# A convolution feeding two feed-forward layers: due dates of five convolutions put two slots earlier, their first step one slot earlier

## Chip, cores and metric

The kernel runs on one core of one Trainium2 chip. The metric is device time in microseconds (us), the median of several executions. One further execution was profiled, and all rows below come from it.

## What is computed

The reference, cut to the arithmetic (the input is 2 x 4096 tokens of 192 channels; all is in float32):

```python
# attn: causal depthwise convolution, 7 taps, softmax-normalised weights, 8 heads
out = np.einsum('hk,bskhg->bshg', w, x_unf)          # x_unf: 7 shifted copies of x
# layer 1, x (8192,192), w_in (192,2048), w_out (2048,192)
h = x @ w_in;  g = h * np.clip(h + 3.0, 0.0, 6.0) / 6.0;  y = g @ w_out
# layer 2, other weights
h = y @ w_in;  g = np.where(h > 0, h, np.exp(np.minimum(h, 0.0)) - 1.0);  out = g @ w_out
```

## The kernel before

**Tiling.** The 8192 tokens are cut into 16 blocks of 512 (256 of each batch entry). The 2048 inner columns of a layer are cut into 16 chunks of 128. One layer, one block and one chunk make a *slot*, `(l, b, f)`, and the list `slots` is the order of the program: first layer-1 blocks 0 and 1 interleaved (slots 0 to 31), then layer-1 blocks 2 to 5 (slots 32 to 95, 16 each), then layer-2 block 0 (96 to 111), layer-1 block 6 (112 to 127), and from there a layer-2 and a layer-1 block in turn, ending with layer-2 blocks alone. `at` gives the number of a slot. BOTH is 32, the first slot of block 2.

**A slot.** TensorE (PE) makes `h` from the block's operands (`mm1`, L452) and four slots later adds this slot's share to the outputs `p` (`mm2`, L492). Between them ScalarE (ACT) makes `u` from `h`, VectorE (DVE) makes the gate `g` from `u` and `h`, ACT rounds `g` to `gh`, and DVE makes the rest `gl = g - gh`. Products are split into high and low parts, so a slot has ten matmuls. From slot 36 on each matmul is done as two halves of 64 rows: the stream of lower halves runs eight matmuls ahead of that of upper halves, and the two alternate in one PE queue. `h` has three PSUM buffers, so `mm1` of slot s needs that `g` of slot s-3 is done.

**The operands.** `mm1` of a layer-1 block reads the tiles opA, opB, opC and opD. `conv(b)` makes them: two DVE transposes of the block's tokens (`squares`: xT from x_sq and xr_sq), twelve multiply-adds on DVE (`acc`, six of 512 and six of 256 columns; ACT starts each sum), then copies on ACT and subtractions on DVE: opA on ACT, opB on DVE, first halves of opC and opD on ACT, their other halves on DVE, then one more ACT copy each. `mm1` reads opA, opB, opA, opC, opD in this order, and an upper or a lower half may leave out one of the last two. The loads of a block's tokens are a job of their own (`feed`), in SyncE's (SP's) queue.

**The order of the work.** Instructions of each engine stand in the order in which the program issues them (up to slot 36 a scheduler may still exchange them; from there the order is as written). Convolutions and the decoding of weights are *jobs*. After the gate of every slot s, `run_jobs(s)` issues steps of those jobs that are wanted. A job has a first slot `a`, a due slot `e` and a number of steps n. It is finished outright once `s >= e - 2` (`e - 1` where e is not over 32); before that its steps are spread evenly, `done * (e - a) < n * (s - a + 1)`. In the slots before 36, instead, steps are issued where a budget of DVE and ACT work allows. For layer-1 block b, `conv(b)` has n = 22 steps, `a = t` and `e`, as set in these lines:

```python
    for b in range(2, NBLK):
        e = at[0, b, 0]
        if b <= RA:
            t = at[0, b - 1, 1]
        else:
            t = at[1, b - RA - 1, NF - 3]
            e = at[1, b - RA, NF - 3]
        job(feed(b), 1, t - 8, t - 7)
        job(whole(squares(b), conv(b)), 2 + CONV, t, e)
```

RA is 6. While layer-1 blocks 2 to 6 are computed, the weights of layer 2 are decoded too, which is more DVE and ACT work in the same slots.

Of the kernel before, what the change touches and what calls it, by code (L numbers as in the profile page):

```python
# [56 lines left out]
def conv_moe_moe2(ctx: ExitStack, tc: tile.TileContext, x, weight, w_in1, w_out1, w_in2, w_out2, out):  # L57
# [211 lines left out]
    def squares(b):  # L269
        for part, t in enumerate(x_sb.pop(b)):  # L270
            vec.transpose(out=halves(b, part), in_=t)
            yield
# [48 lines left out]
    def conv(b):  # L321
        opnd[0, b] = ring()
        yield from alternate(conv_main(b, taps_tensor if b < TENSOR_TAPS else taps_vector), conv_r(b))
# [12 lines left out]
    def feed(b):  # L336
        load_squares(b)
        yield
# [166 lines left out]
    at = {sl: i for i, sl in enumerate(slots)}  # L505
# [11 lines left out]
    def job(gen, n, a, e):  # L517

        jobs.append([e if callable(e) else lambda: e, a, gen, n, 0])
# [29 lines left out]
    def whole(*gens):  # L549
        for g in gens:  # L550
            yield from g
# [105 lines left out]
    job(weights, 0, 0, pace)  # L657
    job(conv(1), CONV, 0, at[0, 1, 0])
    for b in range(2, NBLK):
        e = at[0, b, 0]  # L660
        if b <= RA:
            t = at[0, b - 1, 1]
        else:
            t = at[1, b - RA - 1, NF - 3]
            e = at[1, b - RA, NF - 3]
        job(feed(b), 1, t - 8, t - 7)
        job(whole(squares(b), conv(b)), 2 + CONV, t, e)
    for b in range(NBLK):
        e = at[1, b, 0]
# [100 lines left out]
```

## Time and profile before

| what | us |
|---|---|
| median of three executions | 1200.68 (1200.63 to 1919.79) |
| the profiled execution | 1200.85 |
| its span, first to last instruction | 1199.1 |
| PE busy | 1173.4 (98%) |
| DVE busy | 943.7 (79%) |
| ACT busy | 931.4 (78%) |
| mean granted PE clock | 0.992 of full |

The span is what the rows count in; 1.75 us of the profiled execution lie around it. Busy time of PE is the time in which at least one matmul was shown; it says nothing of how many ran in it. A number in square brackets behind an instruction is the idle time of its engine just before it, and what ended it.

### The profile page before, as it was taken

What the parts mean: (1) busy time and instruction counts of PE and PEld (TensorE: products, weight loads), DVE (VectorE), ACT (ScalarE), POOL (GpSimd) and SP (SyncE); (2) the same over time, 40 slices, a digit from 0 to 9 for tenths busy, and PEclk for the clock granted to TensorE, in tenths of its full rate; (3) what the DMA queues carried; (4) which work ended last, traced back from release to release, by engine and by line L of the source; (5) the groups of instructions that cost most, each with busy time, mean ns of one, the idle gap of its engine ahead of it and who ended that gap; (6) DMA issues with size and microseconds to landing.
All of it is one profiled execution on the core that took longest, in us unless ns stands there. A gap on an engine that the chain in (4) does not pass through costs nothing.

```text
span 1199.1 us, 25137 instructions
## 1 busy us (share of the span) xinstructions
PE 1173.4 (98%) x9496; PEld 975.2 (81%) x9496; DVE 943.7 (79%) x1607; ACT 931.4 (78%) x1683; POOL 44.1 (4%) x490
## 2 busy tenths in 40 slices
PE   8999999999999999999999999999999999999997
PEld 6787677787898879878898778988889888987776
DVE  8999897897877778787787878778787766677774
ACT  6877676779687786968778697887969678888885
POOL 0000000000000000000000000000000000000000
PEclk9999998999999999999999999999999999999999
DMA  6331111100101001010000101001000000000001
GB/s 166 98 97 31 40 32 41 28 1 1 28 1 19 11 1 28 1 28 1 13 16 1 27 2 28 2 7 22 2 15 2 14 1 2 15 15 15 15 11 18
DMA packets 108091, 26.81 MB, mean 22 GB/s; under 512 B 99648, under 2 KB 106816, under 8 KB 107968
## 3 DMA queue, kind: packets, MB, share of 16 engines
q1 hardware_dynamic: 106320, 24.99, 9.9%
q8 instruction: 74, 1.21, 0.4%
q14 instruction: 49, 0.40, 0.1%
q10 hardware_dynamic: 1648, 0.20, 0.1%
HBM read 18.87 MB, written 6.29 MB: 21 GB/s over the span
## 4 chain that ended last, share of the span: by engine, by line
PE 86%; DVE 7%; ACT 5%; issue 1%; DMA 0%; SPq 0%; ACTq 0%; DVEq 0%
PE p L492 44%; PE h L452 41%; ACT u L51 2%; DVE g L51 2%; DVE acc L51 2%; DVE gl L51 2%; ACT gh L51 1%; ACT y L51 1%; PE psc L291 1%; DVE s L51 0%; ACT opC L51 0%; ACT s L51 0%; DMA x_sb<-in_x_dram 0%; DVE cw L51 0%; ACT opD L51 0%
## 5 line engine op out<-in xcount | busy, mean ns | idle before, releaser
L492 PE MATMUL p<-gh,wo 64*128 64x512 f32 (+1 forms) x2976 | 656.5, 394 | 0.2 <-ACT gh L51 0.2
L492 PE MATMUL p<-gl,wo 64*128 64x512 f32 (+1 forms) x1984 | 535.0, 394 | 0.0
L51 DVE SCALAR_TENSOR_TENSOR g<-u,h 128x512 f32<-128x512 f32 x512 | 350.8, 685 | 224.1 <-ACT u L51 220.4
L492 PEld LDWEIGHTS p<-gh,wo 64*128 64x128 f32 (+1 forms) x2976 | 463.1, 186 | 57.7 <-ACT gh L51 0.7
L492 PEld LDWEIGHTS p<-gl,wo 64*128 64x128 f32 (+1 forms) x1984 | 361.8, 186 | 37.9 <-DVE gl L51 0.3
L51 DVE TENSOR_TENSOR gl<-g,gh 128x512 fp32r<-128x512 f32 x512 | 350.5, 685 | 0.4 <-ACT gh L51 0.2
L51 ACT CAST gh<-g 128x512 fp32r<-128x512 f32 x512 | 311.8, 609 | 21.6 <-DVE g L51 21.3
L51 ACT ACTIVATE u<-h,three 128x512 f32<-128x512 f32 x256 | 176.2, 688 | 118.2 <-PE h L452 116.1
L452 PE MATMUL h<-opA,wi1h 64*128 64x512 f32 x512 | 199.7, 395 | 0.3
L452 PE MATMUL h<-opA,wi1l 64*128 64x512 f32 x512 | 199.2, 394 | 0.0
L452 PE MATMUL h<-opB,wi1h 64*128 64x512 f32 x512 | 198.1, 392 | 0.0
L452 PE MATMUL h<-opA,wi0h 64*128 64x512 f32 (+1 forms) x476 | 189.0, 401 | 3.1 <-ACT opA L51 1.7
L51 ACT ACTIVATE u<-h 128x512 f32<-128x512 f32 x256 | 152.6, 596 | 50.6 <-PE h L452 48.3
L452 PE MATMUL h<-opA,wi0l 64*128 64x512 f32 (+1 forms) x476 | 188.3, 399 | 0.0
L452 PE MATMUL h<-opB,wi0h 64*128 64x512 f32 (+1 forms) x476 | 187.0, 396 | 1.3 <-DVE opB L51 1.1
L51 ACT ACTIVATE u<-u 128x512 f32<-128x512 f32 x256 | 161.9, 632 | 8.1
L452 PE MATMUL h<-opC,wi0r 64*128 64x512 f32 (+1 forms) x366 | 144.9, 398 | 7.5 <-ACT opC L51 7.5
L452 PE MATMUL h<-opD,wi1r 64*128 64x512 f32 x384 | 149.3, 392 | 0.0
L452 PE MATMUL h<-opC,wi1r 64*128 64x512 f32 x384 | 149.3, 392 | 0.0
L452 PE MATMUL h<-opD,wi0r 64*128 64x512 f32 (+1 forms) x366 | 144.2, 396 | 0.0
L51 DVE SCALAR_TENSOR_TENSOR acc<-xT,taps,acc 128x256 f32<-128x256 f32 (+1 forms) x180 | 106.7, 602 | 0.6 <-ACT acc L51 0.5
L452 PEld LDWEIGHTS h<-opA,wi0h 64*128 64x128 f32 (+1 forms) x476 | 88.5, 186 | 21.3 <-DVE g L51 7.8
(83 smaller groups left out, 1255.0 us busy)
## 6 DMA issues: line engine op xcount, KB each, us to landing
raw<-in_moe_w_out_dram SPq DMA_DIRECT2D x16, 384.0 KB, 3.1
out_dram<-z SPq DMA_DIRECT2D x186, 32.0 KB, 1.6
raw<-in_moe_w_in_dram SPq DMA_DIRECT2D x7, 512.0 KB, 3.6
x_sq<-in_x_dram SPq DMA_DIRECT2D x112, 32.0 KB, 2.2
raw<-in_moe_w_in_dram SPq DMA_DIRECT2D x8, 256.0 KB, 4.1
xr_sq<-in_x_dram SPq DMA_DIRECT2D x56, 32.0 KB, 2.0
x_sb<-in_x_dram SPq DMA_DIRECT2D x4, 128.0 KB, 2.9
raw<-in_moe_w_in_dram SPq DMA_DIRECT2D x4, 128.0 KB, 4.1
```

The costliest lines, as they stand in the source:

```text
L51: return fn(*args, **kw)
L291: nc.tensor.matmul(ps[:, n * HB:(n + 1) * HB], diag[k], q[:, n, k:k + HB], start=k == 0, stop=k == K - 1)
L452: mm = nc.tensor.matmul(h, k, m[half], start=low and i == 0, stop=high and i == len(todo) - 1)
L492: nc.tensor.matmul(p, k, m[half], start=first and not end and k is not w0l, stop=last and end == 1)
```

## The change

The due slot of a convolution is two less, and for blocks 2 to 6 the first slot is one less. For blocks 7 to 15 `e` is set again in the `else` branch, so nothing changes there.

```diff
     for b in range(2, NBLK):
-        e = at[0, b, 0]
+        e = at[0, b, 0] - 2
         if b <= RA:
-            t = at[0, b - 1, 1]
+            t = at[0, b - 1, 0]
         else:
             t = at[1, b - RA - 1, NF - 3]
             e = at[1, b - RA, NF - 3]
```

What this moves, at three places. Numbers behind names are those of tiles; the same tile can have another number in the two kernels.

DVE at the first slots of block 2, in the kernel before: the last two of the twelve multiply-adds (acc0, acc1), the last steps of the operands, and the next gates. g_1063 is the gate of slot 31 and stands ten multiply-adds above; g_1123 is that of slot 32.

```order
L51 SCALAR_TENSOR_TENSOR acc0_1081<-xT0_1071,taps_96,acc0_1081 128x512
L51 SCALAR_TENSOR_TENSOR acc1_1083<-xT1_1074,taps_96,acc1_1083 128x256
L51 SCALAR_TENSOR_TENSOR cw_1029<-xw_1027,cw_1029 128x512
L51 TENSOR_TENSOR opB_1078<-acc0_1081,opA_1077 128x512
L51 TENSOR_TENSOR opC_1079<-acc1_1083,opD_1080 64x256
L51 TENSOR_TENSOR opD_1080<-acc1_1083,opC_1079 64x256
L51 TENSOR_TENSOR gl_1129<-g_1063,gh_1127 128x512
L51 SCALAR_TENSOR_TENSOR xw_1027<-xw_1027,cw_1029 128x512
L51 TENSOR_SCALAR cw_1156<-raw_957 128x384
L51 TENSOR_TENSOR yr_1158<-s1_1115,yr_1158 128x512
L51 SCALAR_TENSOR_TENSOR g_1123<-u_1124,h_1117 128x512
```

The same place in the changed kernel. Here g_1078 is the gate of slot 30, g_1097 that of slot 31 and g_1123 that of slot 32; eleven multiply-adds stand between the gate of slot 29 and g_1078.

```order
L51 SCALAR_TENSOR_TENSOR acc0_1041<-xT0_1031,taps_96,acc0_1041 128x512
L51 SCALAR_TENSOR_TENSOR acc1_1043<-xT1_1034,taps_96,acc1_1043 128x256
L51 SCALAR_TENSOR_TENSOR g_1078<-u_1079,h_1072 128x512
L51 TENSOR_TENSOR opB_1038<-acc0_1041,opA_1037 128x512
L51 TENSOR_TENSOR opC_1039<-acc1_1043,opD_1040 64x256
L51 TENSOR_TENSOR opD_1040<-acc1_1043,opC_1039 64x256
L51 TENSOR_TENSOR gl_1084<-g_1014,gh_1082 128x512
L51 TENSOR_TENSOR gl_1103<-g_1078,gh_1101 128x512
L51 SCALAR_TENSOR_TENSOR g_1097<-u_1098,h_1091 128x512
L51 TENSOR_TENSOR wi1r_90<-xw_959,wi1r_90 64x4x128
L51 SCALAR_TENSOR_TENSOR cw_1029<-xw_1027,cw_1029 128x512
L51 SCALAR_TENSOR_TENSOR g_1123<-u_1124,h_1117 128x512
```

The convolution moved ahead of the gates of slots 30 and 31, and some decoding (xw_1027, cw_1156) and the sum yr moved behind the gate of slot 32.

DVE ahead of block 3, whose first slot is 48. In the kernel before, g_1597 is the gate of slot 46 and g_1631 that of slot 47.

```order
L51 TENSOR_SCALAR cw_1572<-raw_1152 128x512
L51 TENSOR_TENSOR opB_1254<-acc0_1257,opA_1253 128x512
L51 SCALAR_TENSOR_TENSOR g_1597<-u_1598,h_1551 128x512
L51 TENSOR_TENSOR gl_1603<-g_1559,gh_1601 128x512
L51 TENSOR_TENSOR opC_1255<-acc1_1259,opD_1256 64x256
L51 TENSOR_TENSOR opD_1256<-acc1_1259,opC_1255 64x256
L51 SCALAR_TENSOR_TENSOR g_1631<-u_1632,h_1591 128x512
```

In the changed kernel g_1530 is the gate of slot 44 and g_1566 that of slot 45.

```order
L51 TENSOR_TENSOR opB_1254<-acc0_1257,opA_1253 128x512
L51 SCALAR_TENSOR_TENSOR g_1530<-u_1531,h_1492 128x512
L51 TENSOR_TENSOR gl_1536<-g_1500,gh_1534 128x512
L51 TENSOR_TENSOR opC_1255<-acc1_1259,opD_1256 64x256
L51 TENSOR_TENSOR opD_1256<-acc1_1259,opC_1255 64x256
L51 SCALAR_TENSOR_TENSOR g_1566<-u_1567,h_1524 128x512
L51 TENSOR_TENSOR gl_1572<-g_1530,gh_1570 128x512
L51 TENSOR_SCALAR cw_1579<-raw_1152 128x512
```

The last operand steps moved up past two gates. Ahead of blocks 4 and 5 they move in the same way.

PE at block 2, in the kernel before; p0_517 and p1_518 are outputs of block 1, gh_1046, gh_1067 and gh_1127 belong to slots 29, 30 and 31, and h_1117 is slot 32.

```order
L492 MATMUL p1_518<-gh_1046,wo0_91 128x512
L492 MATMUL p0_517<-gl_1048,wo0_91 128x512
L492 MATMUL p1_518<-gl_1048,wo0_91 128x512
L492 MATMUL p0_517<-gh_1067,wo0_91 128x512 x2
L492 MATMUL p1_518<-gh_1067,wo0_91 128x512
L492 MATMUL p0_517<-gl_1069,wo0_91 128x512
L492 MATMUL p1_518<-gl_1069,wo0_91 128x512
L492 MATMUL p0_517<-gh_1127,wo0_91 128x512 x2
L492 MATMUL p1_518<-gh_1127,wo0_91 128x512
L452 MATMUL h_1117<-opA_1077,wi0h_85 128x512
```

In the changed kernel gh_1082 and gl_1084 belong to slot 29, gh_1101 to slot 30; h_1117 and h_1137 are slots 32 and 33.

```order
L492 MATMUL p1_518<-gh_1082,wo0_91 128x512
L452 MATMUL h_1117<-opA_1037,wi0h_85 128x512
L452 MATMUL h_1137<-opA_1037,wi0h_85 128x512
L452 MATMUL h_1117<-opB_1038,wi0h_85 128x512
L452 MATMUL h_1117<-opA_1037,wi0l_86 128x512
L452 MATMUL h_1137<-opB_1038,wi0h_85 128x512
L452 MATMUL h_1137<-opA_1037,wi0l_86 128x512
L492 MATMUL p0_517<-gl_1084,wo0_91 128x512
```

The first matmuls of block 2 moved ahead of twelve matmuls on slots 29 to 31.

## Rows read from the trace of the kernel before

**Rows 1.** The page's first part: busy us, share of span, instructions.

```profile
PE 1173.4 (98%) x9496; PEld 975.2 (81%) x9496; DVE 943.7 (79%) x1607; ACT 931.4 (78%) x1683; POOL 44.1 (4%) x490
```

**Rows 2.** Stretches between gates: column names, then start:end, length, busy time and instructions.

```profile
core 0: us, PE busy (x) PEld busy (x) DVE busy (x) ACT busy (x) POOL busy (x), PEclk, DMA share, GB/s
94.12:105.06 10.94, 9.19 (x33) 6.73 (x32) 10.10 (x19) 6.46 (x13) 0.00 (x0) 0.85 0.00 1
105.06:144.27 39.21, 35.61 (x265) 27.94 (x265) 33.00 (x60) 27.56 (x52) 1.24 (x14) 0.95 0.26 55
144.27:186.05 41.78, 38.88 (x304) 30.59 (x302) 36.40 (x65) 29.23 (x55) 1.33 (x15) 0.93 0.12 34
186.05:226.05 40.00, 37.45 (x312) 28.84 (x310) 35.34 (x66) 27.79 (x52) 1.51 (x17) 0.99 0.19 40
...
94.12:262.09 167.97, 157.18 (x1212) 123.21 (x1212) 148.14 (x269) 118.37 (x220) 5.48 (x62) 0.96 0.14 31
...
262.09:1152.54 890.45, 889.83 (x7603) 749.53 (x7602) 682.17 (x1112) 712.95 (x1279) 35.25 (x400) 1.00 0.07 11
```

**Rows 3.** All waits of PE after 262.09: us in total, times, longest.

```profile
PE h L452 <- ACT opC L51: 0.4, 1, 0.4
PE p L492 <- ACT gh L51: 0.2, 1, 0.2
```

**Rows 4.** Timeline at block 2: start, length, instruction, idle time before it.

```profile
94.73 5.38 DVE L51 SCALAR_TENSOR_TENSOR acc<-xT,taps,acc 128x512 f32<-128x512 f32 x10
...
95.47 0.86 PE L492 MATMUL p<-gh,wo 128*128 128x512 f32 x3
...
99.74 0.62 ACT L51 CAST opA<-acc 128x512 fp32r<-128x512 f32 x1 [2.60 <-DVE acc L51]
...
100.41 0.96 PE L452 MATMUL h<-opA,wi0h 128*128 128x512 f32 x3 [1.75 <-ACT opA L51]
```

**Rows 5.** Timeline ahead of block 3, DVE and then PE.

```profile
134.03 0.69 DVE L51 SCALAR_TENSOR_TENSOR g<-u,h 128x512 f32<-128x512 f32 x1 [0.40 <-ACT u L51]
...
135.58 0.69 DVE L51 TENSOR_TENSOR opB<-acc,opA 128x512 fp32r<-128x512 f32 x1
137.08 0.69 DVE L51 SCALAR_TENSOR_TENSOR g<-u,h 128x512 f32<-128x512 f32 x1 [0.82 <-ACT u L51]
...
138.28 0.41 DVE L51 TENSOR_TENSOR opC<-acc,opD 64x256 fp32r<-64x256 f32 x1
...
136.32 0.50 PE L452 MATMUL h<-opB,wi0h 64*128 64x512 f32 x1 [0.37 <-DVE opB L51]
...
139.64 0.79 PE L452 MATMUL h<-opC,wi0r 64*128 64x512 f32 x1 [2.59 <-ACT opC L51]
```

**Rows 6.** Timeline ahead of blocks 4 and 5: one gate, then PE.

```profile
176.19 0.69 DVE L51 SCALAR_TENSOR_TENSOR g<-u,h 128x512 f32<-128x512 f32 x1
...
178.60 0.49 PE L452 MATMUL h<-opB,wi0h 64*128 64x512 f32 x1 [0.77 <-DVE opB L51]
...
181.01 0.79 PE L452 MATMUL h<-opC,wi0r 64*128 64x512 f32 x1 [1.68 <-ACT opC L51]
...
222.86 0.49 PE L452 MATMUL h<-opC,wi0r 64*128 64x512 f32 x1 [2.15 <-ACT opC L51]
```

**Rows 7.** Stretches of 10 us, columns as in Rows 2.

```profile
120.00:130.00 10.00, 10.00 (x86) 8.03 (x88) 10.00 (x20) 6.38 (x11) 0.35 (x4) 1.00 0.15 39
130.00:140.00 10.00, 7.03 (x56) 4.92 (x54) 7.90 (x15) 7.91 (x16) 0.26 (x3) 0.97 0.27 61
140.00:150.00 10.00, 10.00 (x76) 7.95 (x76) 7.12 (x14) 5.38 (x12) 0.35 (x4) 0.86 0.13 20
...
180.00:190.00 10.00, 8.98 (x54) 7.12 (x56) 4.01 (x9) 5.44 (x12) 0.27 (x3) 0.66 0.32 69
```

**Rows 8.** Loads of block 4's tokens in SP's queue, and their first reader.

```profile
105.08 2.08 SPq L266 DMA_DIRECT2D x_sq<-in_x_dram  x4
...
148.41 0.70 DVE L51 STREAM_TRANSPOSE xT<-x_sq 128x512 f32<-128x512 f32 x1
```

## Prediction

> **What bounds the kernel now.** I read the busy shares first. PE is busy for 1173.4 of 1199.1 us [rows 1], so at first sight there is little to win. The second view is the length of each block, taken from the first gate of one block to the first gate of the next. From 262.09 to 1152.54 there are 25 blocks in 890.45 us, 35.62 us each, and PE is idle for 0.62 us in all of them [rows 2]. That is a full PE: one block cannot be shorter without fewer matmuls. The list of PE's waits after 262.09 holds two, of 0.4 and 0.2 us [rows 3]. So anything to be won lies before 262.09, where layer-1 blocks 2 to 5 run one behind the other. There block 2 takes 39.21 us, block 3 41.78 and block 4 40.00 [rows 2], which is 3.59, 6.16 and 4.38 us more than 35.62. One more stretch stands out: from the gate of slot 31 to that of slot 32, the first of block 2, 10.94 us pass, where a slot costs about 35.62/16 = 2.2.
>
> The third view is the timeline at the start of each block. PE waits there for the operands that the convolution makes. At block 2 it idles 1.75 us for opA; ACT could not make opA before, since ten multiply-adds had held DVE for 5.38 us [rows 4]. At block 3 it idles 0.37 us for opB and 2.59 for opC [rows 5], at block 4 0.77 and 1.68, at block 5 2.15 [rows 6]. In each case the last operand step stands in DVE's queue behind a gate which itself waited for the next `u`: opC of block 3 runs at 138.28, behind the gate at 137.08 [rows 5]. The operands are late because of their place in the queue, not for want of their inputs.
>
> The fourth view is the clock. In 130 to 140 the granted clock is 0.97, in 140 to 150 0.86, in 180 to 190 0.66 [rows 7]: after the idle time at blocks 3 and 4 PE runs at 1.2 GHz for a while instead of 2.4. The loss is one minus the clock, times the length: (0.03 + 0.14) x 10 = 1.7 us at block 3 and 0.34 x 10 = 3.4 us at block 4.
>
> **What the change does, and its price.** Despite its wording it acts on five convolutions of blocks 2 to 6; for the others `e` is set again. No instruction is added or taken away. The operand steps of blocks 3, 4 and 5 go up by two gates, and the transposes and multiply-adds of each convolution close up by one to two slots. Two slots are 2 x 2.2 = 4.4 us, more than any of the waits. At block 3 the step that now runs at 138.28 would stand just ahead of the gate that ran at 134.03 [rows 5]; PE asked for opC about 139.64 - 2.59 = 137.05. I therefore take these operand waits as gone.
>
> What is late next is the gate. DVE works through its queue in order, so opB, opC and opD, 0.69 + 0.41 and about 0.4 more, or 1.5 us in all, now stand ahead of a gate two slots earlier. Behind that gate waits PE, because `h` has three buffers. Below, the price is nothing if DVE was idle ahead of these gates, and it was, for 0.40 and 0.82 us at 134.03 and 137.08 [rows 5]. Above, it is the whole 1.5 us, since ahead of block 4 the gate at 176.19 follows without any idle time [rows 6]. Also `u` of that slot now stands behind the last ACT copies of opC and opD, which wait for DVE. I take 1.5 - 0.4 = 1.1 us for each block, the bound less the smaller idle time.
>
> Block by block, with 35.62 us of matmuls as the floor:
> - Gate 31 to gate 32 (10.94 us): in the new order eleven multiply-adds, 11 x 0.538 = 5.9 us by the 5.38 for ten, stand between the gates of slots 29 and 30 and begin about two slots sooner. By the old times they begin at about 90.2 and end at 96.1; opA takes 0.62, so PE has it at 96.7 instead of 100.36. PE now reaches block 2 after the high-part matmuls of slot 29, at about 95.47 + 0.7 = 96.2, and waits 0.5 us instead of 1.75. The gate of slot 32 follows after about 5 to 6 us of queue (two gates, three operand steps, two `gl`, decoding), at 102.0 instead of 105.06. This is 3.1 us sooner; but xw, cw and yr, together about 1.5 us, now come behind it. Between nothing less and all of that I take **2.0**.
> - Block 2 (39.21): less 0.37 + 2.59 of idle and 1.7 of clock is 34.55, under the floor. 35.62 + 1.1 = 36.7, a gain of **2.5**.
> - Block 3 (41.78): less 0.77 + 1.68 of idle and the 2.8 us of the clock's loss that lie before 186.05 is 36.5. DVE alone has 36.40 us of work here [rows 2], so DVE is the floor. 36.4 + 1.1 = 37.5, a gain of **4.3**.
> - Block 4 (40.00): less 0.6 for the rest of the slow clock and 2.15 of idle is 37.25; plus 1.1 is 38.3, a gain of **1.7**.
> - Block 6 comes after layer-2 block 0, and no PE wait for its operands is among those of [rows 3] beyond 0.4 us: nothing.
>
> The sum is 2.0 + 2.5 + 4.3 + 1.7 = 10.5 us. Against the profiled execution, 1200.85 (its span and 1.75 us around it), that is 1190.35; the median of the runs stands 0.17 us lower, so **1190.2**. With all floors reached and no gate late the gain is 3.1 + 3.59 + 5.38 + 4.38 = 16.45, or 1184.2.
>
> The loads cost nothing. `feed` is due one slot sooner, but in SP's queue all loads keep their sequence, behind the same weight loads. Block 4's tokens are issued from 105.08 and first read at 148.41 [rows 8]; the 43 us between cover a read one slot, 2.2 us, earlier. Without that cover a transpose would wait and hold all gates behind it.
>
> **A rule weighed against the rows.** PE shows 10.00 us busy from 140 to 150 with 76 matmuls, and the same 10.00 from 120 to 130 with 86 [rows 7]; the clock is 0.86 in the first. The busy share hides this. By idle time alone I would sum 1.75 + 2.96 + 2.45 + 2.15 = 9.3, less four times 1.1, and expect 4.9 us; by lengths of blocks I get 10.5. The Trainium skill, "Perfetto Trace Analysis", section "Identifying the Most-Contended Engine", says that matmul busy share is a bad measure of TensorE's headroom, since pipelined matmuls look smaller in the trace. The trace bears that out here, and I stay with the lengths.
>
> **Rivals.**
> *DVE takes back what it gives.* Over 94.12 to 262.09 DVE has 148.14 us of work in 167.97 [rows 2], and ahead of the block starts it is full: 10.00 of 10 us from 120 to 130 [rows 7]. If it has no slack before the block starts, the operand waits come back as equally long gate waits and the clock falls as before; only the 2.0 us at block 2 stay: 1198.7. The idle times of 0.40 and 0.82 us speak against it. The Trainium skill, "PSUM — Partial Sum Buffer", section "Engine vs sequencer instructions", has VectorE's queue as strictly first in, first out, the rule by which nothing passes the moved steps; the ten multiply-adds in one piece [rows 4] agree.
> *The clock falls all the same.* If a new wait of about 1 us at blocks 3 and 4 is enough to bring the lower level, the 1.7 and 3.4 us stay lost: 10.5 - 5.1 = 5.4, or 1195.3. The 1.75 us wait at block 2 too was followed by a clock of 0.85 over its stretch [rows 2], which speaks for it; the 2.15 us at block 5 left the stretch from 186.05 at 0.99, most of that from before, which speaks against.
> *Slower.* The moved steps delay the gates by their full 1.5 us and the old waits stay in size, because the multiply-adds, now closer together, keep DVE behind PE up to the block start. Four block starts at 1.5 us give 6 us more: 1206.7. It decides on whether DVE still idles ahead of the gate three slots before a block; the 0.40 us at 134.03 is thin, but the rest after the block start (DVE is busy 4.01 of 10 us from 180 to 190 [rows 7]) shows room that such a delay would first have to use up.
>
> **Chances.** The forecast, 1184 to 1195 around 1190.2: 0.60. The clock falls all the same (1195.3): 0.14. DVE takes it back (1198.7): 0.18. Slower (1206.7): 0.08. The range from 1184.2 to 1198.7 takes in the first two and half of the third, about 0.83; the forecast's own range is 1184.2 to 1195.0. Two per cent, about what a measurement of this kernel can tell from no change, is 24 us: all idle and half-speed time before 262.09 does not make that up, so faster by over 2% has 0.01, slower by over 2% (1224.7) 0.02, and within it 0.97.
>
> **What would show it.** Right: no PE wait for opB or opC over 0.5 us at blocks 3 to 5; block lengths near 36.7, 37.5 and 38.3; a clock of 1.00 from 130 to 150 and at block 4; the gate of slot 32 about 3 us sooner; from there to the end the same length as before. Wrong: PE waits for a gate of over 1.5 us at the block starts, or DVE idle ahead of a transpose, for its load.

## The result, and the profile after

The changed kernel takes 1191.27 us (median of three, 1191.26 to 1191.36) against 1200.68. The ratio is 0.9917 with a 95% interval of 0.9898 to 0.9937: 9.4 us sooner, under one per cent but clear of no change. The one execution of the kernel before that took 1919.79 us is left out of the ratio. The forecast was 1190.2 us, with a range of 1184.2 to 1198.7.

The page of the changed kernel: span, then busy time.

```profile
span 1189.5 us, 25142 instructions
...
PE 1168.2 (98%) x9496; PEld 974.6 (82%) x9496; DVE 943.2 (79%) x1607; ACT 929.5 (78%) x1683; POOL 44.4 (4%) x490
```

The work is the same, DVE 943.2 us against 943.7 [rows 1]; the span is 9.6 us shorter. Next, the changed kernel's stretches between the same gates as in [rows 2]: slot 31 to 32, blocks 2, 3, 4, 5, then layer-2 block 0.

```profile
core 0: us, PE busy (x) PEld busy (x) DVE busy (x) ACT busy (x) POOL busy (x), PEclk, DMA share, GB/s
100.13:102.17 2.04, 1.78 (x8) 1.47 (x9) 1.98 (x5) 1.22 (x3) 0.00 (x0) 1.00 0.00 0
...
102.17:140.31 38.14, 36.21 (x277) 28.95 (x277) 34.65 (x66) 28.47 (x56) 1.24 (x14) 1.00 0.22 49
140.31:178.71 38.40, 36.38 (x302) 28.18 (x301) 36.29 (x66) 28.31 (x53) 1.56 (x16) 1.00 0.13 32
178.71:217.30 38.59, 36.83 (x308) 28.45 (x306) 35.55 (x65) 27.64 (x52) 1.43 (x17) 1.00 0.24 52
217.30:253.24 35.94, 35.94 (x312) 29.13 (x310) 33.49 (x62) 27.11 (x51) 1.50 (x16) 1.00 0.01 1
253.24:288.26 35.02, 35.02 (x304) 28.35 (x302) 27.71 (x48) 32.72 (x63) 1.41 (x16) 1.00 0.01 2
```

The reader is to see three things. The granted clock is 1.00 in every stretch, where it was 0.85, 0.95, 0.93 and 0.99 [rows 2]. The gate of slot 112 comes at 288.26 instead of 297.57, so nearly all of the 9.6 us are won before it. And blocks 2, 3 and 4 still take 38.1 to 38.6 us where a full PE needs 35.62.

What PE waits for from 93 to 254 in the changed kernel: us in total, times, longest.

```profile
PE h L452 <- DVE g L51: 5.3, 8, 1.6
PE h L452 <- ACT opA L51: 1.0, 1, 1.0
PE h L452 <- ACT opC L51: 0.4, 1, 0.4
PE p L492 <- DVE gl L51: 0.3, 1, 0.3
```

At blocks 3, 4 and 5 there is no wait for an operand any more; those of [rows 5, 6] are gone. In their place stand gates. The two largest, from the changed kernel's timeline of PE (start, length, instruction, idle time before it):

```profile
117.11 0.50 PE L452 MATMUL h<-opA,wi0h 64*128 64x512 f32 x1 [1.57 <-DVE g L51]
...
174.82 0.49 PE L452 MATMUL h<-opA,wi0h 64*128 64x512 f32 x1 [1.35 <-DVE g L51]
```

Ahead of the second, DVE's timeline in the changed kernel:

```profile
170.37 0.68 DVE L51 SCALAR_TENSOR_TENSOR g<-u,h 128x512 f32<-128x512 f32 x1
...
172.03 0.41 DVE L51 TENSOR_TENSOR opC<-acc,opD 64x256 fp32r<-64x256 f32 x1
172.47 0.42 DVE L51 TENSOR_TENSOR opD<-acc,opC 64x256 fp32r<-64x256 f32 x1
174.08 0.69 DVE L51 SCALAR_TENSOR_TENSOR g<-u,h 128x512 f32<-128x512 f32 x1 [1.18 <-ACT u L51]
```

and ACT's, which explains the 1.18 us:

```profile
172.48 0.41 ACT L51 CAST opD<-opC 64x256 fp32r<-64x256 f32 x1 [3.03 <-DVE opC L51]
172.93 0.41 ACT L51 CAST opC<-opD 64x256 fp32r<-64x256 f32 x1
173.36 0.69 ACT L51 ACTIVATE u<-h,three 128x512 f32<-128x512 f32 x1
```

The last two operand copies stand in ACT's queue ahead of `u`. ACT waits 3.03 us for DVE's opC, makes the copies and only then `u`; the gate waits for `u`, and PE for the gate. The same knot was there before the change, with the same 1.18 us ahead of the gate at 140.33, but two slots later, where PE was waiting for the operand itself.

### The profile page after: what moved, and what is told of

Its sections match the earlier page's. It is cut to its first block, busy times and chain, and to the rows that moved or that the text cites. A ratio compares the mean times of both kernels' runs of the same rounds, so it can differ in the third digit from the quotient of the medians.

```text
span 1189.5 us, 25142 instructions
## 1 busy us (share of the span) xinstructions
PE 1168.2 (98%) x9496; PEld 974.6 (82%) x9496; DVE 943.2 (79%) x1607; ACT 929.5 (78%) x1683; POOL 44.4 (4%) x490
## 4 chain that ended last, share of the span: by engine, by line
PE 85%; DVE 7%; ACT 5%; issue 2%; DMA 0%; SPq 0%; ACTq 0%; DVEq 0%
PE p L492 44%; PE h L452 41%; ACT u L51 2%; DVE g L51 2%; DVE acc L51 2%; DVE gl L51 2%; ACT gh L51 1%; ACT y L51 1%; PE psc L291 1%; DVE s L51 0%; ACT opC L51 0%; ACT yr L51 0%; ACT opD L51 0%; ACT xw L51 0%; ACT s L51 0%
## 5 line engine op out<-in xcount | busy, mean ns | idle before, releaser
L452 PE MATMUL h<-opA,wi1h 64*128 64x512 f32 x512 | 200.0, 395 | 0.3
L452 PE MATMUL h<-opA,wi1l 64*128 64x512 f32 x512 | 199.5, 394 | 0.0
L452 PE MATMUL h<-opB,wi1h 64*128 64x512 f32 x512 | 198.6, 393 | 0.0
L452 PE MATMUL h<-opA,wi0h 64*128 64x512 f32 (+1 forms) x476 | 189.6, 401 | 6.7 <-DVE g L51 5.3
L452 PE MATMUL h<-opA,wi0l 64*128 64x512 f32 (+1 forms) x476 | 188.3, 398 | 0.0
L452 PE MATMUL h<-opB,wi0h 64*128 64x512 f32 (+1 forms) x476 | 186.3, 393 | 0.0
L452 PE MATMUL h<-opC,wi1r 64*128 64x512 f32 x384 | 149.5, 393 | 0.0
L452 PE MATMUL h<-opD,wi1r 64*128 64x512 f32 x384 | 149.5, 393 | 0.0
L452 PE MATMUL h<-opC,wi0r 64*128 64x512 f32 (+1 forms) x366 | 143.6, 393 | 1.0 <-ACT opC L51 1.0
L452 PE MATMUL h<-opD,wi0r 64*128 64x512 f32 (+1 forms) x366 | 143.4, 393 | 0.0
L452 PEld LDWEIGHTS h<-opA,wi0h 64*128 64x128 f32 (+1 forms) x476 | 88.0, 185 | 26.6 <-DVE g L51 14.0
```

The lines of the kernel that those rows point to most:

```text
L452: mm = nc.tensor.matmul(h, k, m[half], start=low and i == 0, stop=high and i == len(todo) - 1)
```

## The experiments

The theory at the start: operands came late because of their place in VectorE's queue; the due slot moves that place; the price is gate waits, because VectorE is nearly full. The rivals: the earlier first step is what counts; VectorE's load makes the operands late; block 2 alone, or only the others, carry the gain. Times are medians; the kernel before was timed again beside each of three groups of runs (1200.29, 1200.59 and 1200.19 us).

### Which part of the change, and which blocks

Due slots alone, first slots as before:

```diff
-        e = at[0, b, 0]
+        e = at[0, b, 0] - 2
```

> The due slots of blocks 2 to 6 are two less, the first slots as before. Theory: the gain comes from the place of the last operand steps in VectorE's queue, which the due slot alone sets. Then this is 1190.5 to 1192.5 us (the changed kernel has 1191.27, the kernel before 1200.68), TensorE waits for no opB or opC over 0.7 us at blocks 3 to 5, and the granted clock stays at 1.00 after 94 us. Rival: the earlier first step is what makes room; then this stays above 1196.

Measured: 1190.83 us (ratio 0.9927, 0.9912 to 0.9942). The theory holds: the due slot alone brings the whole gain. PE's waits are 5.1 us for gates and none for opB or opC at blocks 3 to 5, and the granted clock is 1.00 from 94 to 262.

First slots alone:

```diff
-            t = at[0, b - 1, 1]
+            t = at[0, b - 1, 0]
```

> The first slots of blocks 2 to 6 are one less, the due slots as before. Theory: the operand steps keep their place, so the waits at blocks 3 to 5 stay within 1 us of 2.96, 2.45 and 2.15, the clock falls again, and the time is 1198 to 1202 us. Rival (the earlier start makes the room): below 1196.

Measured: 1197.28 us (0.9975, 0.9964 to 0.9987), just under the theory's range. PE's waits from 94 to 262 in this kernel:

```profile
PE h L452 <- ACT opC L51: 6.1, 3, 2.3
PE h L452 <- ACT opA L51: 1.7, 1, 1.7
PE h L452 <- DVE g L51: 1.2, 1, 1.2
PE h L452 <- DVE opB L51: 0.7, 1, 0.7
```

The waits for opC stay (6.4 us before), as they should where the operand steps keep their place. The time goes with the clock: its ten runs reach from 1194.83 us at a mean clock of 0.997 to 1199.32 at 0.993, and the profiled one is the slowest of them. The same spread is in the kernel before, 1198.22 at 0.995 to 1202.25 at 0.991 over 33 further runs, and hardly with due slots alone (1190.73 to 1191.09, clock 0.998 to 0.999). So the earlier first slot is worth 3 us by itself, and nothing once the due slots are two earlier.

Block 2 alone, and all but block 2:

```diff
-        e = at[0, b, 0]
+        e = at[0, b, 0] - 2 * (b == 2)          # the other: 2 * (b > 2)
-            t = at[0, b - 1, 1]
+            t = at[0, b - 1, int(b > 2)]        # the other: int(b == 2)
```

> Both changes for block 2 alone. Theory: the gate of slot 32 comes 2.9 us sooner, as in the changed kernel (102.17 against 105.06), and the waits at blocks 3 to 5 stay; 1197 to 1199 us. Rival: what is won at block 2 is given back in the same block, since decoding moves behind its first gate; then 1200 to 1201.

> Both changes for blocks 3 to 6, block 2 as before. Theory: the shares add up, so this is the changed kernel plus what block 2 alone is worth: 1193 to 1195 us; the wait of 1.75 us for opA at block 2 and the half clock after it stay, and the clock stays at 1.00 at blocks 3 and 4. Rival: block 2 sets the pace of what follows, and the waits at block 3 come back; then above 1197.

Measured: block 2 alone 1200.0 us (0.9999, 0.9989 to 1.0008), no gain; all but block 2 1191.23 us (0.993, 0.9913 to 0.9946), the whole gain. Both times the theory failed: I had expected 2 to 3 us from block 2, and they are not there. With block 2 alone the gate of slot 32 does come early, at 102.01 against 105.06. But an early gate is not yet time won. PE's timeline at this place, in the changed kernel:

```profile
95.45 0.86 PE L492 MATMUL p<-gh,wo 128*128 128x512 f32 x3
97.31 0.73 PE L452 MATMUL h<-opA,wi0h 128*128 128x512 f32 x2 [1.00 <-ACT opA L51]
...
99.54 0.50 PE L492 MATMUL p<-gl,wo 128*128 128x512 f32 x1 [0.31 <-DVE gl L51]
100.39 0.50 PE L452 MATMUL h<-opC,wi0r 128*128 128x512 f32 x1 [0.35 <-ACT opC L51]
...
106.42 0.50 PE L452 MATMUL h<-opA,wi0h 64*128 64x512 f32 x1
```

and with all but block 2 changed:

```profile
95.42 0.86 PE L492 MATMUL p<-gh,wo 128*128 128x512 f32 x3
100.36 0.96 PE L452 MATMUL h<-opA,wi0h 128*128 128x512 f32 x3 [1.75 <-ACT opA L51]
...
106.40 0.49 PE L452 MATMUL h<-opA,wi0h 64*128 64x512 f32 x1
```

Both lists begin with the matmuls on gh of slot 29 and end with the first half matmul, that of slot 36. Up to there the same 35 matmuls run, in another order, and PE is equally far at the end, 106.42 against 106.40. It waits 1.00 + 0.31 + 0.35 = 1.66 us in the first and 1.75 in the second. The gate of slot 32 is early only because block 2's first matmuls moved ahead of twelve on slots 29 to 31, which now come behind it. The stretches to block 3's first gate, all but block 2 changed:

```profile
94.07:104.30 10.23, 8.43 (x34) 5.92 (x33) 10.11 (x20) 6.51 (x14) 0.00 (x0) 1.00 0.00 1
104.30:140.31 36.01, 34.08 (x267) 26.96 (x267) 32.86 (x61) 27.68 (x54) 1.23 (x14) 1.00 0.23 52
```

The gate of slot 32 comes 2.1 us later than in the fully changed kernel and the block is 2.1 us shorter, so it ends at the same 140.31. The rival of the first run named a time that fits (1200 to 1201), but not the cause: nothing was won that could be given back. In its profiled run the kernel with block 2 alone is still 1.7 us ahead at block 3's first gate (142.59 against 144.27), mostly because the clock did not fall at block 2 there (1.00 against 0.86 from slot 29's matmuls to slot 36); it then fell at block 5, to 0.83 from 220 to 230.

### One piece of work at slot 36

In the changed kernel the steps that fall due in slots 32 to 36 are issued in one piece at slot 36, where the even spreading begins. DVE then runs, ahead of one gate:

```profile
112.69 0.70 DVE L51 STREAM_TRANSPOSE xT<-x_sq 128x512 f32<-128x512 f32 x1
113.32 0.41 DVE L51 STREAM_TRANSPOSE xT<-xr_sq 128x256 f32<-128x256 f32 x1
114.25 2.21 DVE L51 SCALAR_TENSOR_TENSOR acc<-xT,taps,acc 128x512 f32<-128x512 f32 x4 [0.52 <-ACT acc L51]
116.37 0.68 DVE L51 SCALAR_TENSOR_TENSOR g<-u,h 128x512 f32<-128x512 f32 x1
```

That is the gate for which PE waited 1.57 us at 117.11; in the kernel before two of these multiply-adds stand there, and PE waits 0.51 us. I took the piece for the place where block 2 gives back its gain. It is not: with all but block 2 changed, PE waits the same 1.58 us at 117.11. But it is the largest gate wait, and the next kernel takes it apart:

```diff
-            t = at[0, b - 1, 0]
+            t = at[0, b - 1, 4 * (b == 3)]
```

> The changed kernel with block 3's first slot at 36 instead of 32. In the changed kernel the steps of slots 32 to 36 come in one piece at slot 36: two transposes and four multiply-adds ahead of one gate, and TensorE waits 1.57 us for that gate at 117.11. Theory: this piece, and not the operands of block 2, sets the end of block 2 (102.17 to 140.31); here the wait falls under 0.6 us and the time to 1189.5 to 1190.7 us. Rival: VectorE's total load in block 2 sets it, and the multiply-adds come back as waits later in the block; then 1191 to 1192.

Measured: 1191.98 us (0.9933, 0.9919 to 0.9948), not faster than the changed kernel; the rival holds. The wait at 117 is gone, but PE's timeline in this kernel has three others in its stead:

```profile
128.03 0.49 PE L452 MATMUL h<-opA,wi0h 64*128 64x512 f32 x1 [0.60 <-DVE g L51]
...
130.76 0.50 PE L452 MATMUL h<-opA,wi0h 64*128 64x512 f32 x1 [0.36 <-DVE g L51]
...
136.43 0.50 PE L452 MATMUL h<-opA,wi0h 64*128 64x512 f32 x1 [0.96 <-DVE g L51]
```

0.60 + 0.36 + 0.96 = 1.92 us stand for the 1.57 and one of 0.23 at 135.84 in the changed kernel. Taken out of one place, DVE's work in block 2 comes back as waits at others.

### Place in the queue, or load

Here four of the six multiply-adds of each sum are left out for the convolutions of blocks 3 to 6, in the kernel before and in the changed one; all other instructions keep their slots.

```diff
         for k in range(1, K):
-            vec.scalar_tensor_tensor(out=a, ...)
+            if k < 3 or b < 3 or b > RA:
+                vec.scalar_tensor_tensor(out=a, ...)
             yield
```

> The kernel before, with four of the six multiply-adds of each sum left out for the convolutions of blocks 3 to 6 (their steps stay as empty steps, so the other instructions keep their slots): about 8 x 0.54 = 4.3 us less VectorE work in each of blocks 2 to 4. Theory: operands are late by their place in the queue, behind gates that wait for TensorE itself, and not by VectorE's load; the waits for opB and opC at blocks 3 to 5 stay, at least 1.5 us at each of two of them, and the time is at least 1195 us. Rival: VectorE's load makes them late; then the waits are gone and the time is within 1.5 us of that of the next run.

> The changed kernel with the same multiply-adds left out. Theory: what remains above 35.62 us a block in the changed kernel (38.14, 38.40 and 38.60 for blocks 2 to 4) is VectorE's load, shown as gate waits; with 4.3 us less of it blocks 3 and 4 take 35.6 to 36.5 us and the time is 1184 to 1187.5. Rival: the rest comes from the order of the ACT copies ahead of u and stays; then above 1189.

Measured: 1191.9 us with the old due slots (0.9925, 0.991 to 0.994), 1185.88 with the new ones (0.9877, 0.986 to 0.9893). PE's waits from 102 to 262 with the old due slots and less load (L453 there is L452 of the other kernels):

```profile
PE h L453 <- ACT opC L51: 5.0, 3, 2.0
PE h L453 <- DVE g L51: 0.5, 1, 0.5
```

DVE has 3.8 to 3.9 us less work in each of blocks 2 to 4 (4.3 by the estimate). Three waits for opC stay, 2.00, 1.33 and 1.70 us, against 2.59, 1.68 and 2.15; the two for opB, 1.1 us, are gone. Of 7.6 us of operand waits 5.0 stay: this load makes a third of them, and the place in the queue, which the due slot alone moves, the rest. The expected time of at least 1195 us was wrong: the waits are shorter, and in the profiled run the clock fell only once, after the wait of 2.00 us. With the new due slots and the lighter load the stretches of blocks 2, 3 and 4 are:

```profile
102.07:138.65 36.58, 35.01 (x273) 29.07 (x273) 30.93 (x58) 27.72 (x54) 1.42 (x14) 1.00 0.23 51
138.65:175.67 37.02, 35.91 (x308) 30.77 (x305) 32.30 (x57) 28.69 (x55) 1.58 (x16) 1.00 0.12 33
175.67:211.65 35.98, 35.83 (x308) 28.69 (x306) 31.59 (x58) 27.10 (x52) 1.42 (x17) 1.00 0.26 56
```

They are 1.4 to 2.6 us shorter each than in the changed kernel. At blocks 3 and 4, 4.0 of the 5.7 us that were left above 35.62 are thus VectorE's load, as the theory has it. Block 3, at 37.02, is above the expected 36.5: DVE idles 1.18 us there for a `u` behind the same two ACT copies as in the changed kernel, load or no load.

### How far ahead

```diff
-        e = at[0, b, 0] - 2
+        e = at[0, b, 0] - 1                     # the other: - 4
```

> As the changed kernel, with the due slots one less instead of two: operands come 2.2 us sooner than before, where the waits were 2.96, 2.45 and 2.15 us. Theory: up to 0.8 us of operand wait stay at block 3, less at the others; 1191 to 1195 us. Rival (any wait at a block start brings the lower clock): above 1195.

> As the changed kernel, with the due slots four less. Theory: at two slots the operand waits are gone, so two more slots win nothing; the multiply-adds stand closer together and delay more gates, 0 to 2 us: 1191 to 1193.5 us. Rival: the margin at two slots is still what costs (operands late in some blocks): 1188 to 1190.

Measured: one slot 1187.75 us (0.9892, 0.9877 to 0.9907), four slots 1192.78 (0.9934, 0.9919 to 0.9949). Four slots are in the theory's range. One slot is better than two by 3.5 us, which neither side expected. PE's waits with one slot (93 to 254):

```profile
PE h L452 <- ACT opC L51: 2.6, 4, 1.1
PE h L452 <- DVE g L51: 2.4, 3, 1.6
PE h L452 <- ACT opA L51: 0.7, 1, 0.7
```

At blocks 3, 4 and 5 the waits for opC are 0.25, 1.05 and 0.80 us; the theory had the largest at block 3. With four slots (93 to 256):

```profile
PE h L452 <- DVE g L51: 8.1, 11, 2.9
```

Operand waits fall with every slot ahead: 9.2 us before (1.7 for opA, 1.1 for opB, 6.4 for opC), 3.3 with one slot, 1.4 with two, none with four. Gate waits rise: 1.0, 2.4, 5.3 and 8.1 us. The sum is smallest at one slot, 5.7 us against 6.7 with two. That is 1.0 of the 3.5 us. Part of the rest are waits that no list holds. A half matmul is shown for 0.39 us, but the next of its stream starts 0.23 us after it where nothing holds it up, so the first tenths of a wait are shown as busy. In the changed kernel the gates at 155.56 and 158.03 end at 156.25 and 158.72, and PE's next matmuls of a new slot start 0.05 to 0.06 us after each, without a wait in brackets:

```profile
156.31 0.49 PE L452 MATMUL h<-opA,wi0h 64*128 64x512 f32 x1
...
158.77 0.49 PE L452 MATMUL h<-opA,wi0h 64*128 64x512 f32 x1
```

How much of the 2.5 us these make was not added up.

Three more kernels, all with due slots one less, vary the first slot:

```diff
-            t = at[0, b - 1, 0]
+            t = at[0, b - 1, 4 * (b == 3)]        # due1_spread3
+            t = at[0, b - 1, 1]                   # due1_oldstart
+            t = at[0, b - 1, 4 if b > 2 else 1]   # due1_late
```

> Due slots one less (1187.75 us as it stands) and block 3's first slot at 36. Theory: the gain of the run before adds to that of the smaller due change: 1186.2 to 1187.2 us. Rival: 1187.5 to 1188.5.

> Due slots one less, first slots as in the kernel before. Theory: the first slot is worth under 1 us either way, as with due slots two less (1190.83 against 1191.27); 1186.8 to 1188.5 us. Rival: the one-slot earlier start is what lets one slot suffice; then above 1189.

> Due slots one less, first slots of blocks 3 to 6 four slots into the block before. Theory: at the start of a block VectorE also adds up the block before (y, s, yr, about 2 us); starting later takes the transposes out of that piece but sets the multiply-adds closer, so the two about cancel: 1186 to 1188.5 us, with the clock at 1.00. Rival: the closer multiply-adds make the operands late again: above 1189, with waits for opC over 1 us.

Measured: 1187.46, 1188.88 and 1191.69 us (0.9896, 0.9908 and 0.9931, each within 0.0017). The first falls between the two expectations: no more than 0.3 us, not settled. The second is 0.4 us over the theory's range and below the rival's: with one slot the earlier start is worth about 1 us, with two it was not. The third goes to the rival by its time: started four slots later, the operands are late again. But PE waits longest for opB, and no wait for opC is over 0.5 us. PE's waits in it from 93 to 254:

```profile
PE h L452 <- DVE opB L51: 2.5, 3, 0.9
PE h L452 <- DVE g L51: 2.3, 5, 1.2
PE h L452 <- ACT opC L51: 1.9, 4, 0.5
PE h L452 <- ACT opA L51: 0.7, 1, 0.7
```

Due slots one ahead, with the first slots of the change, give the best version but for those 0.3 us: 1187.75 us, faster than both kernels.

## Why the prediction was right, step by step

**Operand waits go.** Right. At blocks 3, 4 and 5 none is left, and the due slot alone does it. The reading behind it holds in full only for block 3. At blocks 4 and 5 the gate just ahead of opC (178.46 and 219.83 in the kernel before) follows without idle time, and part of the waits is load.

**The clock stays up.** Right, and it is the larger share. By lengths and clock, the kernel before lost up to 1.6 + 1.7 + 3.4 = 6.7 us to half speed from 94 to 262 (0.15 x 10.94 at block 2, and [rows 7]), the changed kernel nothing. PE's listed waits in the same part fell from 10.2 to 7.0 us, so 3.2. Together 9.9, of which 262.09 - 253.24 = 8.9 us are seen at the first gate of layer 2. The 6.7 are a little too many: the 35 matmuls at block 2 took 1.1 us longer than in the kernel that has the same wait at full clock (107.54 against 106.40), not 1.6.

**New gate waits of 1.1 us a block.** Right in kind, too small. Gate waits rose from 1.0 to 5.3 us, or 4.3 in three blocks: 1.4 each, close to the upper bound of 1.5. At 174.82 the cause is the one named, the moved steps and the ACT copies ahead of `u`. The largest, 1.57 us at 117.11, has another that the prediction does not name: the steps of block 3's convolution that come in one piece at slot 36.

**Block 2's start, 2.0 us.** Wrong. The gate of slot 32 came at 102.17, as worked out (102.0), 2.9 us sooner than before; but block 2 then takes 38.14 us where I had put 36.7. The step that failed is to count the early gate as time won. I charged it with the decoding that comes behind it, and not with the matmuls of block 1 that do, so the floor of 35.62 us is too low for block 2 as counted from this gate (PE is shown busy for 36.21). Nor did PE's wait shrink from 1.75 to 0.5 us: with those for gl and opC it is 1.66. The kernel that leaves block 2 alone is as far at slot 36 and reaches block 3's first gate at the same 140.31. That the two terms, 2.0 + 2.5, still became 144.27 - 140.31 = 4.0 us there is luck in part: 1.1 us of it is the half clock behind the wait for opA, which was in no term of the sum, and the rest is won at block 3's operands and their clock.

**Blocks 3 and 4 at 37.5 and 38.3.** Measured 38.40 and 38.59: gains of 3.4 and 1.4 us instead of 4.3 and 1.7. Gate waits undersized by 0.4 us at each account for block 4; the other half of block 3's shortfall was not traced.

**Nothing after block 4.** Slightly wrong. Block 5 is 0.1 us shorter, layer-2 block 0 0.5 (35.02 against 297.57 - 262.09 = 35.48), where the wait of 0.4 us for opC of block 6 [rows 3] is gone, and the rest 0.3.

The forecast sum was 10.5 us: too large by 0.5 for block 2 and its start, by 0.9 and 0.3 for blocks 3 and 4, and short of 0.9 after them. That gives the 9.6 to 9.7 of the spans; the agreement to 1.1 us owes something to the last, and to the half clock at block 2.

**The rivals.** That DVE takes back what it gives is true in part: 4.3 us came back as gate waits. That the clock falls all the same did not happen: gate waits of 1.57 and 1.35 us left it at 1.00. That new waits of this length must do so is not shown (see the last section). The slower case did not come: the moved steps cost nearly their full price, but the old waits did go. What the Trainium skill says in "Perfetto Trace Analysis", section "Identifying the Most-Contended Engine", on matmul busy share was borne out: PE's share is 98% before and after, with 9.6 us between them, and the forecast by idle time alone, 4.9 us, would have missed half. The reason that the Trainium skill gives there, that pipelined matmuls look smaller, is not what is seen here: from 140 to 150 the share is full with 76 matmuls shown instead of 86, and short waits count as busy.

## What to carry to other kernels

Where an engine works through its queue in order, a due time is a place in that queue: moving it earlier trades waits for the moved result against waits for everything it now stands ahead of. The best of the places tried here (none, one, two and four slots) is the one with the smallest sum, one slot and not two. Measure the neighbours of a change in due time, not only the change. An event that comes sooner is not time won where an engine only takes up its work in another order: compare two kernels at a point behind which the same work is left.

## What had not been expected of the hardware

The clock does not answer equal waits in the same way. The wait of 1.75 us for opA at block 2 was followed by half speed in the profiled run of the kernel before (0.85 over its stretch, [rows 2]); the same wait in the kernel that leaves block 2 alone was not (1.00 in 94.07 to 104.30, above). The wait of 2.15 us at block 5 left the clock at 1.00 in the kernel before; with block 2 alone changed, a wait of 2.16 us there was followed by 0.83 from 220 to 230. The longest of all is a gate wait in the kernel with due slots four less, and the clock is 1.00 from there to 130:

```profile
117.00 0.50 PE L452 MATMUL h<-opA,wi0h 64*128 64x512 f32 x1 [2.89 <-DVE g L51]
```

So the length of a wait alone does not tell whether the clock falls, and what does stays open. The four kernels with the old due slots at blocks 3 to 5, where waits of 1.3 to 2.6 us for opC stand, vary by 2.6 to 4.5 us from run to run, along with the mean clock; all others by 0.6 us or less.
